# Scores of three row blocks in one TensorE visit, and values in one tile of 576 columns

## The chip, the cores and the metric

The kernel runs on one core of a Trainium2 chip. The metric is the device time of one execution in microseconds, as the median of several runs. Each core has a matrix engine (TensorE, PE), three engines for elementwise work (VectorE or DVE, ScalarE or ACT, GpSimd or POOL) and a queue engine (SyncE, SP) that only issues DMAs here. Each engine takes its instructions in the order in which they are laid out and waits at semaphores for the others. TensorE writes to PSUM alone, eight banks of 512 fp32 columns over 128 partitions.

## The reference

Forgetting attention (causal softmax attention with a decay of the scores) is followed by a bilinear feed-forward network (FFN):

```python
B, H, S, D = 8, 8, 576, 64
scores = (q @ k.T) / 8 + cum[:, :, :, None] - cum[:, :, None, :]   # cum = cumsum(log(clip(f)))
scores = where(causal, -1e9, scores)                                # above the diagonal
attn = exp(scores - max); attn /= sum(attn)
x = (attn @ v) put as (B * S, H * D)                                # 4608 tokens of 512
out = ((x @ w_a) * (x @ w_b)) @ w_out                               # d_ff = 1536
```

## The kernel before

**Work.** All of it is on one core, in fp16 with fp32 sums. Attention goes by pairs of heads: pair t covers batch t // 4 and heads t % 4 and t % 4 + 4, so there are 32 pairs. A pair's 576 query rows are four blocks of 128 (0 to 3) and a last one of 64 (block 4, both heads in one tile). Block i needs 128 (i + 1) columns of keys a head.

**Stages of a pair.** TensorE computes scores (`qk_group`). For blocks 0 to 3 it uses 64-row matmuls, the two heads in the two halves of the array (64\*128 in the profile); for block 4 of later pairs it uses queries laid out over 128 rows (64 columns wide, 128\*64). VectorE adds the decay and takes the row minimum of the negated sum in one custom operation (`do_decay`, L580) from PSUM into a buffer S. ScalarE takes the exponential with its row sum (`do_exp`, L611 and L607). VectorE takes reciprocals, GpSimd normalizes (`do_norm`, L629). SyncE's queue issues DMA transposes of the weights: PA (blocks 0 to 2) into PTA and PB (blocks 3 and 4) into PTB (`do_tr`, L643). TensorE multiplies them with the values (`do_pv` for blocks 0 to 3, L671, `do_pv4` for the last 64 rows, L687), and VectorE evicts the result into xT (L267 and L698). Batch 0 and, in part, batch 1 (pairs 0 to 7) go by other paths: their decay is added by TensorE or in other layouts, and transposes go through TensorE (`psP`).

**FFN.** Tokens go in groups of 256, 256, 256, 384, six of 512, and 384. Each of the twelve 128-column blocks of d_ff takes eight matmuls for `psa` and eight for `psb` (128\*64, two halves of the array); ScalarE copies `psa`, VectorE multiplies `psb` with it into `ht`. Then `pso` sums twelve blocks per 128 tokens; it is copied and stored. A group can start when the values of its batches stand in xT.

**PSUM before.** `sc` has two tiles of two banks, for scores, taken in turn. `pv` is one bank for values. `ff` is a ring of three banks for psa, psb, pso and the results of TensorE's transposes (psT for q and k, psP), in an order given by the table `FFBANK`. The last 64 value columns of pair t - 2 are written into spare columns of pair t's first score tile, so values of pair t - 2 stand behind pair t's first scores and are evicted in two parts (512 and 64 columns).

**Order.** All operations are objects with dependencies; `ORDER` lists them in one sequence written out by hand or by a planner, and each engine gets its share of it. `CHOICE` says, for operations that may run on one of several engines, which takes them. 24 operations `wake` (four matmuls each) on TensorE fill gaps at the start.

The lines in question before:

```python
c = ps.tile([128, 2, 512], FP32, tag="sc", bufs=2, name=f"sc{g}")           # L454, scores of one group
for gs in ([(0,), (1,), (2, 3)] if b in EARLY else [(0,), (1,), (2,), (3,)]):   # L757
pv = ... do_pv(old, (0, 1, 2, 3), {"A", "B"}), do_pv4(old, T.pop(("spare", t)))  # L790, old = t - 2
groups = [(1, 0), (2,), (3,), (4,)]                                         # L700
```

Of the kernel before, what the change touches and what calls it, by code (L numbers as in the profile page):

```python
# [25 lines left out]
def kernel(  # L26
# [76 lines left out]
    def paddings():  # L103
# [6 lines left out]
        for i in range(2):  # L110
# [13 lines left out]
            "sc": 2, "qd": 2, "pv": 1, "ff": 3}  # L124
# [54 lines left out]
    def f_tiles():  # L179
        x = [s_pool.tile([128, 1024], FP32, tag="S", name=n) for n in ("cum_f", "cum_l")]  # L180
        cw["f"], cw["l"] = (t[:, 0:S] for t in x)
        cw["1"] = x[0][:, S:].bitcast(FP16)[:, 0:S]
# [39 lines left out]
    for n in range(24):  # L222
        o = Op("PE", 0.427, lambda _: wake(2), [o_i], prio=-290, mode="full", name=f"wake{n}")
        o.prev = [last_wake] if n else []
        last_wake = o
        take(o, "pv")
# [42 lines left out]
    def load_v(b, sbs):  # L269
        x = T[("v32", b, sbs[0])] = n32_pool.tile([128, 2 * TG * 64], FP32, tag="n32", name="v32")  # L270
# [11 lines left out]
    def load_qk(b, which, half):  # L282
# [3 lines left out]
        if b in EARLY:  # L286
            if b == 0 and half:
                n = 2 * TG * 64
                x = wout16.rearrange("p n k -> p (n k)")[:, n * (which == "q"):n * (which == "q") + n]
                x = x.rearrange("p (j t d) -> p j t d", j=2, t=TG)  # L290
            else:
                x = n16_pool.tile([128, 2, TG, 64], FP16, tag="n16", name=f"{which}16")
# [3 lines left out]
        x = n32_pool.tile([128, 2 * TG * 64], FP32, tag="n32", name=f"{which}32")  # L296
# [4 lines left out]
    def cast_qk(e, b, which, half, lo, hi):  # L301
        key = ("n16", which, b, half)
        if key not in T:
            T[key] = n16_pool.tile([128, TG, 2, 64], FP16, tag="n16", name=f"{which}16")
# [145 lines left out]

    def qk_group(t, g):
        b, pr = divmod(t, NP)
        qT, kT = T[("T", "q", b)], T[("T", "k", b)]
        c = ps.tile([128, 2, 512], FP32, tag="sc", bufs=2, name=f"sc{g}")  # L454
# [28 lines left out]
        if g == 0:  # L483
            T[("spare", t)] = c[:, 0, 448:512]
# [64 lines left out]
    def do_max(t, i):  # L549
        if ("st", t) not in T:  # L550
            T[("st", t)] = st_pool.tile([128, 32], FP32, tag="st", name="st")
# [4 lines left out]
    def do_decay(t, g, i, h):  # L556

        if ("st", t) not in T:
            T[("st", t)] = st_pool.tile([128, 32], FP32, tag="st", name="st")
        if ("S", t, g) not in T:  # L560
            T[("S", t, g)] = s_pool.tile([128, 1024], FP32, tag="S", name="S")
# [9 lines left out]
        else:  # L571
            n = 128 * (i + 1)
            o, x, y = T[("z", t, i)][:, h * n:h * n + n], T[("s", t, i)][:, h, :], c[:, h, SM:SM + n]
# [16 lines left out]
    def p_blocks(t, i):  # L590
# [3 lines left out]
        else:  # L594
            if ("P", "A", t) not in T:
                T[("P", "A", t)] = p_pool.tile([128, 12, 128], FP16, tag="PA", bufs=RING["PA"], name="PA")
# [61 lines left out]
    def do_pv(t, rows, parts):  # L658
# [3 lines left out]
        o = ps.tile([128, 512], FP32, tag="pv", bufs=1, name="pv")  # L662
# [13 lines left out]
    def do_pv4(t, o=None):  # L676
# [4 lines left out]
        own = o is None  # L681
        if own:
            o = ps.tile([128, 512], FP32, tag="pv", bufs=1, name="pv4")[:, 0:64]
        T[("pv4", t)] = o
        for j in range(NSB):
            for h in range(2):
                nc.tensor.matmul(out=o[HP[h], :], lhsT=vt[:, j, pr + NP * h, :],  # L687
                                 rhs=pb[:, 8 + j, 64 * h:64 * h + 64], start=own and (j == 0),
                                 stop=(j == NSB - 1), skip_group_check=True)

# [24 lines left out]

    LAG = 2

    def attention(t, base):
# [36 lines left out]
        qk_of, sc_of, spare_pv = {}, {}, []  # L755
        qk_prev = None
        for gs in ([(0,), (1,), (2, 3)] if b in EARLY else [(0,), (1,), (2,), (3,)]):  # L757
# [5 lines left out]
            def stage(_, gs=gs):  # L763
                for g in gs:
# [11 lines left out]
            elif qk_prev:  # L776
                qk.deps.append(qk_prev)
            elif b not in EARLY and (t - 1, 3) in qk_ops:
                qk.prev.extend([qk_ops[(t - 1, 2)], qk_ops[(t - 1, 3)]])
            qk_prev = qk  # L780
            for g in gs:
                qk_of[g], sc_of[g] = qk, take(qk, "sc")
# [4 lines left out]
            old = t - LAG  # L787
            if gs == (0,) and b not in EARLY and old // NP not in EARLY:
                pv = Op("PE", 10 * 128 * COLS * 1.05 + 0.15,
                        lambda _, old=old: (do_pv(old, (0, 1, 2, 3), {"A", "B"}), do_pv4(old, T.pop(("spare", t)))),  # L790
                        [qk, *late[old][0]], prio=prio(0), mode="col", name=f"pv{old}")
                sc_of[0].append(pv)
                spare_pv.append(pv)
                late[old][1](pv, sc_of[0])
        direct_ex = {}
        for g, gi in [(g, groups[g]) for g in ((0, 1, 3, 2) if t in MASKP else (0, 1, 2, 3))]:
            qk, sc, su = qk_of[g], sc_of[g], None
            for i in gi:
                part = part_of(t, i)
                mxs = []  # L800
                for h in range(1 if direct else 2):
# [6 lines left out]
                    if g == 0 and spare_pv:  # L808
                        spare_pv[0].deps.append(mx)
# [15 lines left out]
                    sc.append(mx)  # L825
# [89 lines left out]
        def pv_late(pv, sc0):  # L915
            pvu = take(pv, "pv")
            p = pv.prio - 1
            ev = Op("DVE", 0.69, lambda e: do_ev(e, t, (0, 1, 2, 3)), [pv], prio=p, name=f"ev{t}")
            pvu.append(ev)
            ev4 = Op("DVE", 0.22, lambda _: do_ev4(t), [pv], prio=p)  # L920
            sc0.append(ev4)
# [3 lines left out]
            for i in range(NSB):  # L925
                ev_ops[(t, i)] = ev4 if i == 4 else ev

        if b not in EARLY and t + LAG < NP * B:
            late[t] = [o for x in sorted(trs) for o in trs[x]] + v_ops[b], pv_late
            return  # L930
        for rows in ([(0, 1), (2, 3)] if b in EARLY else [(0, 1, 2, 3)]):
# [6 lines left out]
            pvu = take(pv, "pv")  # L938
# [9 lines left out]
        pvu4 = take(pv4, "pv")  # L948
        ev4 = Op("DVE", 0.22, lambda _: do_ev4(t), [pv4], prio=p - 1)
# [15 lines left out]
    def ff_copy(e, t0, n, fb):  # L965
        a16 = a16_pool.tile([128, 512], FP16, tag="a16", name="a16")
# [3 lines left out]
    def ff_mul(t0, n, fb):  # L970
        ht = ht_pool.tile([128, 512], FP16, tag="ht", name="ht")
# [12 lines left out]
    def ff_ocopy(e, t0, tb):  # L984
        osb = osb_pool.tile([128, 512], FP32, tag="osb", name="osb")
# [3 lines left out]
    def last_copy(e, t0, tb, part):  # L989
        x = T[("half", part)] = s_pool.tile([128, 1024], FP32, tag="S", name="half")  # L990
# [86 lines left out]
    for n in cuts:  # L1077
# [3 lines left out]
        0 1 45 2 49 28 29 4-8 46 9 10 30-33 36 37 47 48 50 51 35 38 34 39 11 53 57 3 78 61 65 63 42 54  # L1081
# [6 lines left out]
        104 272 233 72 142 103 386 1750-1752 145 1753 201 202 150 1754-1757 108 25 146 151 1758 387 1760  # L1088
# [9 lines left out]
        339 438 368 361 362 494-496 314 315 320 505 488 500 1803 1804 373 1805 506 360 489 497 363 364  # L1098
# [156 lines left out]
```

## Time and profile before

| | us |
|---|---|
| median of 3 runs | 405.65 |
| lowest and highest | 405.36, 406.97 |
| profiled execution, its own time | 406.14 |
| its span, first to last instruction | 404.4 |
| TensorE busy | 389.1 (96%) |
| VectorE busy | 298.2 (74%) |
| ScalarE busy | 283.6 (70%) |
| GpSimd busy | 262.3 (65%) |

The profile names groups by line, engine, operation, and output and input tiles: `sc<-kT,qT` are scores, `psT` transposes of q and k, `pv<-PTA,nv` and `pv<-PTB,nv` values, `sc<-PTB,nv` the last 64 value columns in the spare part of a score tile, `psa`, `psb` and `pso` the FFN. A timeline line gives the start, the length, the engine, the line, the operation, the shape (for TensorE rows\*columns of the weights, then the moving operand) and the count; in square brackets stand idle time before it and what ended it. Matmuls are pipelined, so that lengths overlap and starts are the better measure. A line of waits gives microseconds in total, times, and the longest.

### The profile page before, as it was taken

Reading aid. Unit: us, or ns where it says so; the run is one execution under the profiler, and the core shown is the slowest. Engines: PE = TensorE matmul, PEld = TensorE weight load, DVE = VectorE, ACT = ScalarE, POOL = GpSimd, SP = SyncE. Lnnn points to the kernel's source line nnn. Section 1 sums busy time; section 2 is a strip of 40 time slices with the busy share of each in tenths; the row PEclk is TensorE's granted clock in tenths of the full one; section 3 lists DMA queues with packets and bytes.
Section 4 is the critical chain, followed back from the end, with each engine's and each line's share of the span. In section 5 each row is a group of like instructions: output and inputs, shape, how many; then the busy total and the mean of one; then the engine's idle time right before and its main releaser. Section 6 shows DMA issues by size and latency. Waiting matters only on the chain.

```text
span 404.4 us, 14858 instructions
## 1 busy us (share of the span) xinstructions
PE 389.1 (96%) x5792; PEld 240.6 (60%) x5792; DVE 298.2 (74%) x1003; ACT 283.6 (70%) x801; POOL 262.3 (65%) x489
## 2 busy tenths in 40 slices
PE   6899799999999999999999997999999999999995
PEld 2457586877956656555555554555555555555663
DVE  3777888999888888876897786788979882541331
ACT  2998889989988778887786867587788762231330
POOL 8897579968789687967698756875786573000000
PEclk9999999999999999999999999999999999999999
DMA  8999968999999999999999999999996496101102
GB/s 141 218 176 178 192 144 178 218 261 278 285 208 216 302 229 231 282 237 228 243 252 275 227 182 296 186 247 229 225 226 140 85 191 141 67 2 53 54 2 78
DMA packets 147190, 76.88 MB, mean 190 GB/s; under 512 B 124336, under 2 KB 129200, under 8 KB 147120
## 3 DMA queue, kind: packets, MB, share of 16 engines
q1 hardware_dynamic: 141040, 68.73, 76.9%
q0 software_dynamic: 5936, 7.08, 10.7%
q8 instruction: 45, 0.74, 0.8%
q14 instruction: 25, 0.20, 0.2%
q10 hardware_dynamic: 144, 0.13, 0.1%
HBM read 52.05 MB, written 9.58 MB: 152 GB/s over the span
## 4 chain that ended last, share of the span: by engine, by line
PE 65%; DMA 3%; DVE 2%; ACT 0%; issue 0%; ACTq 0%; DVEq 0%
PE pso L74 19%; PE psa L74 18%; PE psb L74 18%; PE sc L457 4%; PE pv L671 3%; DMA PTB<-PB 2%; PE sc L74 1%; PE psT L315 1%; DMA out_dram<-osb 1%; DVE S L580 1%; PE sc L687 1%; DVE osb L267 0%; DVE ht L972 0%; ACT osb L263 0%; DVE half L267 0%
## 5 line engine op out<-in xcount | busy, mean ns | idle before, releaser
L580 DVE CUSTOM_DVE_ANT_0 S<-sc,spread 64x576 f32<-64x576 f32 (+4 forms) x232 | 125.4, 562 | 14.0 <-PE sc L457 4.0
L74 PE MATMUL psa<-xT,wa 128*64 128x512 f16 (+2 forms) x1056 | 116.6, 342 | 1.8 <-DVE qT L265 1.3
L74 PE MATMUL psb<-xT,wb 128*64 128x512 f16 (+2 forms) x1056 | 116.3, 341 | 0.0
L263 ACT CAST a<-psa 128x512 f16<-128x512 f32 (+2 forms) x132 | 66.6, 504 | 59.2 <-PE psa L74 49.4
L629 POOL TENSOR_SCALAR PA<-PA,st 128x128 f16<-128x128 f16 (+2 forms) x192 | 89.8, 478 | 24.8 <-DVE st L621 16.0
L972 DVE TENSOR_TENSOR ht<-psb,a 128x512 f16<-128x512 f32 (+2 forms) x132 | 77.2, 589 | 33.5 <-PE psb L74 28.7
L74 PE MATMUL pso<-wout,ht 128*64 128x512 f16 x864 | 100.8, 380 | 0.0
L611 ACT ACTIVATE PA<-S,st 128x256 f16<-128x256 f32 (+2 forms) x168 | 84.4, 504 | 6.4 <-DVE st L580 6.0
L629 POOL TENSOR_SCALAR PB<-PB,st 128x512 f16<-128x512 f16 (+1 forms) x96 | 67.5, 710 | 21.6 <-DVE st L619 9.5
L74 PEld LDWEIGHTS <-wa 128*64 128x64 f16 x1056 | 58.3, 110 | 35.6 <-issue 4.5
L74 PEld LDWEIGHTS <-wb 128*64 128x64 f16 x1056 | 58.0, 110 | 31.6 <-issue 1.9
L74 PEld LDWEIGHTS <-ht 128*64 128x64 f16 x864 | 47.0, 110 | 37.5 <-issue 1.0
L611 ACT ACTIVATE PB<-S,st 128x512 f16<-128x512 f32 x56 | 40.1, 718 | 2.7 <-DVE st L580 2.4
L457 PE MATMUL sc<-kT,qT 64*128 64x128 f16 (+4 forms) x384 | 33.8, 266 | 1.5 <-ACT qT L261 1.1
L611 ACT ACTIVATION_READ_ACCUMULATOR PA<-S,st 128x1 f32 x168 | 32.0, 190 | 0.0
L267 DVE CAST xT<-pv 128x512 f16<-128x512 f32 (+1 forms) x40 | 23.0, 575 | 10.2 <-PE pv L671 10.1
L607 ACT ACTIVATE PB<-S,st 128x576 f16<-128x576 f32 x28 | 21.6, 772 | 9.5 <-POOL PA L629 5.7
L671 PEld LDWEIGHTS <-nv 128*64 128x64 f16 x640 | 21.9, 110 | 8.8 <-issue 4.4
L457 PEld LDWEIGHTS <-qT 64*128 64x128 f16 (+1 forms) x384 | 13.1, 95 | 19.8 <-issue 12.0
L580 DVE CUSTOM_DVE_ANT_1 S<-sc,spread 128x256 f32<-128x256 f32 x48 | 19.7, 419 | 5.3 <-PE sc L457 2.2
L263 ACT COPY osb<-pso 128x512 f32<-128x512 f32 x18 | 10.3, 575 | 18.2 <-PE pso L74 18.2
L580 DVE DVE_READ_ACCUMULATOR2_ANT st<- 128x1 f32 (+1 forms) x280 | 22.9, 82 | 0.0
(100 smaller groups left out, 465.1 us busy)
## 6 DMA issues: line engine op xcount, KB each, us to landing
spread<-cum_d SPq DMA_DIRECT2D x24, 576.0 KB, 6.3
out_dram<-osb SPq DMA_DIRECT2D x35, 256.0 KB, 3.4
v<-in_v_dram SPq DMA_DIRECT2D x32, 256.0 KB, 5.0
q<-in_q_dram SPq DMA_DIRECT2D x12, 576.0 KB, 5.4
k<-in_k_dram SPq DMA_DIRECT2D x12, 576.0 KB, 5.9
wout<-in_moe_w_out_dram POOLq DMA_DIRECT2D x3, 512.0 KB, 7.2
v<-in_v_dram SPq DMA_DIRECT2D x8, 128.0 KB, 7.5
wa<-in_moe_w_a_dram POOLq DMA_DIRECT2D x2, 512.0 KB, 8.7
```

The costliest lines, as they stand in the source:

```text
L74: nc.tensor.matmul(out=out[r], lhsT=lhsT[:, r], rhs=rhs, **kw)
L263: nc.scalar.copy(out=out_, in_=in_)
L267: VEC[e].tensor_copy(out=out_, in_=in_)
L315: nc.tensor.matmul(out=p[m][HP[j] if b in EARLY else slice(0, 128), 64 * t:64 * t + 64], lhsT=x[r, j, t, :] if b in EARLY else x[r, t, :], ...
L457: nc.tensor.matmul(out=dst, lhsT=lhsT, rhs=rhs, start=start, stop=stop, skip_group_check=True)
L580: nc.vector.tensor_tensor_reduce(out=o, in0=x, in1=y, scale=-1.0, scalar=3e38, op0=ADD, op1=MIN, accum_out=m)
L607: nc.scalar.activation(out=p_blocks(t, 4), in_=T[("s" if direct else "z", t, 4)], func=EXP, bias=st[:, 8:9], scale=sign, accum_out=st[:, 1 ...
L611: nc.scalar.activation(out=p_blocks(t, i)[:, :, h, :], in_=(T[("s", t, i)][:, h, :] if direct else T[("z", t, i)][:, h * n:h * n + n]).rea ...
L629: VEC[e].tensor_scalar(out=p, in0=p, scalar1=st[:, c:c + 1], scalar2=1.0, op0=MUL, op1=MUL)
L671: nc.tensor.matmul(out=o[HP[h], 128 * i:128 * i + 128], lhsT=vt[:, j, pr + NP * h, :], rhs=pt[:, base_blk[i] + 2 * block_at(t, i, j) + h, ...
L687: nc.tensor.matmul(out=o[HP[h], :], lhsT=vt[:, j, pr + NP * h, :], rhs=pb[:, 8 + j, 64 * h:64 * h + 64], start=own and (j == 0), stop=(j = ...
L972: nc.vector.tensor_tensor(out=ht[:, 0:n], in0=T.pop(("psb", t0, fb))[:, 0:n], in1=T.pop(("a16", t0, fb))[:, 0:n], op=MUL)
```

## The change

From batch 2 on (pairs 8 to 31):

- `qk_first` computes the scores of blocks 0, 1 and 2 in one visit of ten matmuls. Blocks 0 and 2 stand in a two-bank `sc` tile, one bank a head, and block 1 in two `ff` ring banks, one a head. Block 3 and block 4 keep a tile and a visit each.
- Values of all 576 columns go into one two-bank `sc` tile (`do_pv_all`), are no longer tied to the first scores two pairs on, and are evicted by one operation (`do_ev_all`), on VectorE or ScalarE as `CHOICE` says: 9 on VectorE, 15 on ScalarE.
- The separate `pv` bank goes; the `ff` ring has four banks, which `wake` and the values of pairs 0 to 7 use too.
- Which buffer a tile takes is read from tables (`SLOTS`) for PSUM and for S, PA, n32, n16, st, a16, ht and osb, instead of turn about. The counts of these buffers stay.
- `ORDER` and `CHOICE` are new throughout. Among GpSimd's instructions the first two loads of w_b stand ahead of the k and q loads of batch 1.

```diff
     def wake(n):
-        x = ps.tile([128, 512], FP32, tag="pv", bufs=1, name="wake")
+        x = ff_tile([128, 512], FP32, "wake")
...
-            "sc": 2, "qd": 2, "pv": 1, "ff": 3}
+            "sc": 2, "qd": 2, "ff": 4}
...
-    ff_bank = []
+    SLOTS = """
+        PA:03210231023102310231023102310231;S:010101011010101001010101010101010100101110000100101010111101011100
...
+    """
+    slot_of = {x.split(":")[0]: list(x.split(":")[1]) for x in "".join(SLOTS.split()).split(";") if x}
+
+    def slot(p, shape, dtype, tag, name):
+        return p.tile(shape, dtype, tag=tag + slot_of[tag].pop(0), bufs=1, name=name)
 
     def ff_tile(shape, dtype, name):
-        return ps.tile(shape, dtype, tag=f"ff{ff_bank.pop(0)}", bufs=1, name=name)
+        return slot(ps, shape, dtype, "ff", name)
...
+    def qk_first(t):
+        b, pr = divmod(t, NP)
+        qT, kT = T[("T", "q", b)], T[("T", "k", b)]
+        c = slot(ps, [128, 2, 512], FP32, "sc", "sc0")
+        c1 = [ff_tile([128, 512], FP32, f"sc1{h}")[:, 0:256] for h in range(2)]
+        out_of = {0: [c[:, h, 0:128] for h in range(2)], 1: c1, 2: [c[:, h, 128:512] for h in range(2)]}
+        for i in (1, 0, 2):
+            for x, (j0, j1) in enumerate(key_runs(t, i)):
+                for h, r in enumerate(HP):
+                    w, col = 128 * (j1 - j0), 128 * x
+                    nc.tensor.matmul(out=out_of[i][h][:, col:col + w], lhsT=qT[r, pr, 128 * i:128 * i + 128],
+                                     rhs=kT[r, pr, 128 * j0:128 * j1], start=i < 2 and x == 0 , stop=True,
+                                     skip_group_check=True)
+        for i in range(3):
+            T[("s", t, i)] = out_of[i]
...
-        if g == 0:
-            T[("spare", t)] = c[:, 0, 448:512]
...
+    def do_pv_all(t):
+        o = T[("pvx", t)] = slot(ps, [128, 2, 512], FP32, "sc", "pvx").rearrange("p a k -> p (a k)")
+        do_pv(t, (0, 1, 2, 3), {"A", "B"}, o)
+        do_pv4(t, o[:, SF:S])
+
+    def do_ev_all(e, t):
+        b, pr = divmod(t, NP)
+        cast(e, xT[pr][:, b, :], T.pop(("pvx", t))[:, 0:S], False)
...
-    LAG = 2
...
-        for gs in ([(0,), (1,), (2, 3)] if b in EARLY else [(0,), (1,), (2,), (3,)]):
+        for gs in ([(0,), (1,), (2, 3)] if b in EARLY else [(0, 1), (2,), (3,)]):
...
+            if gs == (0, 1):
+                u = take(qk, "sc")
+                users_of.update({0: u, 2: u, 1: (take(qk, "ff"), take(qk, "ff"))})
...
-            old = t - LAG
-            if gs == (0,) and b not in EARLY and old // NP not in EARLY:
-                pv = Op("PE", 10 * 128 * COLS * 1.05 + 0.15,
-                        lambda _, old=old: (do_pv(old, (0, 1, 2, 3), {"A", "B"}), do_pv4(old, T.pop(("spare", t)))),
-                        [qk, *late[old][0]], prio=prio(0), mode="col", name=f"pv{old}")
...
+        if b not in EARLY:
+            p = prio(0) - 1
+            pv = Op("PE", 0.7, lambda _: do_pv_all(t), [o for x in sorted(trs) for o in trs[x]] + v_ops[b], prio=p, mode="col", name=f"pv{t}")
+            pvu = take(pv, "sc")
+            ev = Op(None, {"DVE": 0.75, "ACT": 0.78}, lambda e: do_ev_all(e, t), [pv], prio=p, name=f"ev{t}")
...
-            pvu = take(pv, "pv")
+            pvu = take(pv, "ff")
...
     ORDER = """
...
     CHOICE = """
...
-    FFBANK = """
...
```

More of the change, by code (lines that the diff above doesn't have):

```diff
@@ L179, in f_tiles @@
     def f_tiles():
-        x = [s_pool.tile([128, 1024], FP32, tag="S", name=n) for n in ("cum_f", "cum_l")]
+        x = [slot(s_pool, [128, 1024], FP32, "S", n) for n in ("cum_f", "cum_l")]
         cw["f"], cw["l"] = (t[:, 0:S] for t in x)
@@ L291, in load_qk @@
             else:
-                x = n16_pool.tile([128, 2, TG, 64], FP16, tag="n16", name=f"{which}16")
+                x = slot(n16_pool, [128, 2 * TG * 64], FP16, "n16", f"{which}16").rearrange("p (j t d) -> p j t d", j=2, t=TG)
             T[("n16", which, b, half)] = x
@@ L295, in load_qk @@
             return
-        x = n32_pool.tile([128, 2 * TG * 64], FP32, tag="n32", name=f"{which}32")
+        x = slot(n32_pool, [128, 2 * TG * 64], FP32, "n32", f"{which}32")
         x = x.rearrange("p (j t d) -> p j t d", j=2, t=TG)
@@ L303, in cast_qk @@
         if key not in T:
-            T[key] = n16_pool.tile([128, TG, 2, 64], FP16, tag="n16", name=f"{which}16")
+            x = slot(n16_pool, [128, 2 * TG * 64], FP16, "n16", f"{which}16")
+            T[key] = x.rearrange("p (t h d) -> p t h d", t=TG, h=2)
         cast(e, T[key][:, lo:hi].rearrange("p t h d -> p h t d"), T[("n32", which, b, half)][:, :, lo:hi, :], which == "q")
@@ L680, in do_pv4 @@
         vt = nv[b % 2]
-        own = o is None
-        if own:
-            o = ps.tile([128, 512], FP32, tag="pv", bufs=1, name="pv4")[:, 0:64]
+        if o is None:
+            o = ff_tile([128, 512], FP32, "pv4")[:, 0:64]
         T[("pv4", t)] = o
@@ L775, in attention @@
                 qk.deps.append(cp)
-            elif qk_prev:
+            elif b in EARLY and qk_prev:
                 qk.deps.append(qk_prev)
-            elif b not in EARLY and (t - 1, 3) in qk_ops:
-                qk.prev.extend([qk_ops[(t - 1, 2)], qk_ops[(t - 1, 3)]])
             qk_prev = qk
+            if gs == (0, 1):
+                u = take(qk, "sc")
+                users_of.update({0: u, 2: u, 1: (take(qk, "ff"), take(qk, "ff"))})
             for g in gs:
-                qk_of[g], sc_of[g] = qk, take(qk, "sc")
+                qk_of[g] = qk
+                if gs != (0, 1):
+                    u = take(qk, "sc")
+                    users_of.update({i: u for i in groups[g]})
                 qk_ops[(t, g)] = qk
@@ L925, in pv_late @@
             for i in range(NSB):
-                ev_ops[(t, i)] = ev4 if i == 4 else ev
-        if b not in EARLY and t + LAG < NP * B:
-            late[t] = [o for x in sorted(trs) for o in trs[x]] + v_ops[b], pv_late
+                ev_ops[(t, i)] = ev
             return
-        for rows in ([(0, 1), (2, 3)] if b in EARLY else [(0, 1, 2, 3)]):
+        for rows in [(0, 1), (2, 3)]:
             parts = {part_of(t, i) for i in rows}
@@ L989, in last_copy @@
     def last_copy(e, t0, tb, part):
-        x = T[("half", part)] = s_pool.tile([128, 1024], FP32, tag="S", name="half")
+        x = T[("half", part)] = slot(s_pool, [128, 1024], FP32, "S", "half")
         cast(e, x[:, 0:256], T[("pso", t0, tb)][:, 256 * part:256 * part + 256], False)
```

127 lines of the change are left out of this document (67 added, 60 removed), and 178 rows, old and new, of the table ORDER.

## The prediction

> **What bounds the kernel now.** I read the page first, then the busy times by stretch, TensorE's waits, its timeline, and the chain that ended last.
>
> ```profile
> span 404.4 us, 14858 instructions
> PE 389.1 (96%) x5792; PEld 240.6 (60%) x5792; DVE 298.2 (74%) x1003; ACT 283.6 (70%) x801; POOL 262.3 (65%) x489
> PEclk9999999999999999999999999999999999999999
> PE 65%; DMA 3%; DVE 2%; ACT 0%; issue 0%; ACTq 0%; DVEq 0%
> ```
>
> TensorE (PE) is busy 96% of the span, always at full clock, and is nearly all of the chain that ended last. Where it is not busy, the stretches show:
>
> ```profile
> core 0: us, PE busy (x) PEld busy (x) DVE busy (x) ACT busy (x) POOL busy (x), PEclk, DMA share, GB/s
> 0.00:20.00 20.00, 14.84 (x278) 7.32 (x278) 11.71 (x27) 12.49 (x35) 17.32 (x51) 1.00 1.02 179
> 20.00:50.00 30.00, 26.97 (x592) 18.87 (x586) 24.60 (x62) 25.97 (x77) 23.38 (x41) 1.00 1.04 179
> 120.00:160.00 40.00, 40.00 (x598) 25.06 (x594) 33.30 (x122) 32.35 (x93) 31.32 (x57) 1.00 1.11 248
> 240.00:280.00 40.00, 37.84 (x516) 21.47 (x514) 31.44 (x115) 29.36 (x85) 28.24 (x51) 1.00 1.04 236
> 360.00:380.00 20.00, 20.00 (x198) 11.47 (x196) 5.44 (x9) 4.47 (x8) 0.00 (x0) 1.00 0.14 53
> ```
>
> Of the 15.3 us idle, 8.2 lie in the first 50 us and about 4 behind the last matmul; in the long middle TensorE stands still once, at 240 to 280. VectorE (DVE), the busiest of the others, has 33.3 of 40 us there. So TensorE's order sets the pace, and an edit is worth what it takes from TensorE's own time, plus the waits that it opens or closes:
>
> ```profile
> PE wake L74 <- POOL ident masks.py:199: 2.9, 1, 2.9
> PE pv L671 <- DMA PTB<-PB: 2.1, 1, 2.1
> PE psa L74 <- DVE qT L265: 1.3, 1, 1.3
> PE pv L671 <- issue: 1.2, 1, 1.2
> PE sc L457 <- ACT qT L261: 1.1, 2, 0.9
> ```
>
> **Part 1: the visits.** "Busy" hides a loss, and the timeline shows it by its start times (the durations overlap):
>
> ```profile
> 195.59 1.06 PE L74 MATMUL psa<-xT,wa 128*64 128x512 f16 x8
> 196.58 0.51 PE L457 MATMUL sc<-kT,qT 64*128 64x128 f16 x10
> 197.01 1.05 PE L74 MATMUL psb<-xT,wb 128*64 128x512 f16 x8
> 197.90 1.03 PE L74 MATMUL psa<-xT,wa 128*64 128x512 f16 x8
> 198.76 1.03 PE L74 MATMUL psb<-xT,wb 128*64 128x512 f16 x8
> ...
> 104.35 0.34 PE L457 MATMUL sc<-kT,qT 64*128 64x128 f16 x4
> 104.52 0.43 PE L315 MATMUL psT<-ident,q 64*128 64x64 f16 x18
> ...
> 112.56 0.34 PE L457 MATMUL sc<-kT,qT 64*128 64x128 f16 x6
> 112.74 0.43 PE L315 MATMUL psT<-ident,k 64*128 64x64 f16 x18
> ```
>
> An FFN product of eight matmuls takes 0.86 us when its own kind follows (197.90 to 198.76). Four score matmuls take 0.17 us (104.35 to 104.52) and six 0.18, where other 64-row work follows. From 195.59 to 197.90 lie two products (1.73) and ten score matmuls (0.35), that is 2.08 us of work in 2.31: going over to the 64-row shape and back costs 0.23 us a visit.
>
> In TensorE's order of instructions I counted how often 64-row work (scores of blocks 0 to 3, transposes of q and k) begins behind 128-row work: 82 times before and 68 after, of which 55 and 44 from pair 8's first scores on. Blocks 0, 1 and 2 now come as one visit of ten matmuls where they were often two (six and four). The number of matmuls is the same in both, 5,792, so nothing else of TensorE's work changes. Eleven visits in the paced stretch give 11 x 0.23 = 2.5 us. The other three lie where TensorE also waits for others; they are worth 0 to 0.7, and I take 0.4, since the stretch from 20 to 50 us is already 90% busy. Sum: -2.9 us, with ends at -2.5 and -3.2. [...]
>
> Values and the last rows' scores cost no such switch:
>
> ```profile
> 190.07 1.03 PE L74 MATMUL psb<-xT,wb 128*64 128x512 f16 x8
> 190.94 0.33 PE L671 MATMUL pv<-PTA,nv 128*64 128x128 f16 x6
> ...
> 191.65 1.03 PE L74 MATMUL psa<-xT,wa 128*64 128x512 f16 x8
> ```
>
> The product before them lasts 0.87, and all thirty value matmuls take 0.71 us. One 576-column tile holds the same thirty: 0 on TensorE.
>
> **Part 2: where values stand, and the one long wait.**
>
> ```profile
> 244.03 0.36 PE L671 MATMUL pv<-PTA,nv 128*64 128x128 f16 x6
> 246.45 0.25 PE L671 MATMUL pv<-PTB,nv 128*64 128x128 f16 x2 [2.06 <-DMA PTB<-PB]
> ...
> 237.43 8.97 DMA PTB<-PB
> ```
>
> Pair 21's values start at 244.03, and their transposed second half lands only at 246.4: the 2.1 us above. Before, values of a pair had to follow the first scores two pairs on, because their last 64 columns lay in those scores' tile. The change drops that tie. Counting FFN groups of eight matmuls between a pair's last scores and its values, the order has 19.5 on average (18 for pair 21, least 12) before, and 25.0 (25 for pair 21, least 16) after. Seven more groups at 0.86 are 6 us of cover for a wait of 2.1, so I take the wait as gone: -2.1, with ends 0 (the softmax of the pair slips as far) and -2.1. Pair 31, with 12 groups, had no such wait, so 16 to 35 should do. What is late next, where values come later, is the FFN that needs them: in the counted order the last values of a batch stand between one and four product groups ahead of the first FFN product on that batch's rows, before between one and eight. One group, 0.86, just covers an eviction of 0.64 to 0.75 (below), so I put no price on it beyond the new waits of part 3.
>
> **Part 3: banks and evictions.** The separate value bank becomes a fourth ring bank, but each pair now takes two ring banks for block 1, and values take a two-bank score tile.
>
> ```profile
> L580 DVE CUSTOM_DVE_ANT_1 S<-sc,spread 128x256 f32<-128x256 f32 x48 | 19.7, 419 | 5.3 <-PE sc L457 2.2 <-issue 1.5 <-ACT PB L611 1.0
> L267 DVE CAST xT<-pv 128x512 f16<-128x512 f32 x24 | 16.3, 681 | 7.8 <-PE pv L671 7.8
> L698 DVE CAST xT<-sc 128x64 f16<-128x64 f32 x22 | 4.9, 222 | 6.7 <-PE sc L687 6.4
> L263 ACT COPY kT<-psT 128x576 f16<-128x576 f16 x26 | 15.8, 641 | 3.7 <-PE psT L315 3.5
> L267 DVE COPY kT<-psT 128x576 f16<-128x576 f16 x6 | 4.5, 750 | 0.3 <-PE psT L315 0.3
> ```
>
> VectorE loses two evictions a pair (0.681 and 0.222) and gets 9 of the 24 new ones, at about 0.75 by the nearest row of 576 columns; ScalarE gets 15 at about 0.64. That is 24 x 0.90 - 9 x 0.75 = 15 us less on VectorE and 15 x 0.64 = 10 more on ScalarE. Both lie beside TensorE's work: 0 on the path, and if that cover were gone, 0.64 to 0.75 a pair. A block-1 bank is free after its 419 ns pass. What is queued behind the wait for it is the FFN product, transposes or scores that take that bank next, and everything after them on TensorE. In the order, the tightest block-1 tile has 0.7 us of TensorE work before its bank is wanted again, counted by the durations of what stands between; but FFN tiles already lived with 0.77 before. I expect some short new waits, and bound them by 0 and by the one long wait of the old order, 2.1; I take the middle, +1.0. The scratch and output buffers (S, PA, n16, ht and so on) keep their count and go by a table instead of turn about: 0, since no engine instruction comes with it, and the waits that it could shift are in the same +1.0.
>
> **Part 4: the start.** GpSimd now issues two wb loads (256 and 512 KB) ahead of the first k and q of batch 1:
>
> ```profile
> k<-in_k_dram POOLq DMA_DIRECT2D x3, 288.0 KB, 5.3
> wb<-in_moe_w_b_dram POOLq DMA_DIRECT2D x2, 512.0 KB, 7.1
> ```
>
> Both k and q are transposed just before pair 0's blocks 3 and 4, some 10 us after their issue, against 5.3 us to land, or up to 12.4 if they queue wholly behind wb. The transposes keep TensorE in order, so a late q holds those scores. On the other side, the q transposes of batch 1's second half are now followed by transposes that do not take their bank, where the old order had 1.3 us of FFN waiting for the qT eviction. I take 0, between -2.5 (the waits of 1.3 and 1.2 both go) and +2 (the late load).
>
> **The sum.** -2.9 - 2.1 + 1.0 + 0 = -4.0 us against the profiled execution: span 404.4, its own time 406.14, hence 402.1. The median of the runs shown, 405.65, is 0.5 below that execution, so I forecast 401.6 us.
>
> **The rivals.**
>
> - *The gain is hidden.* TensorE leaves its visits sooner, but the softmax of the next pair arrives as before, so the time shows up as waits on transposes. For it: the wait at 244 shows that the pair's pipeline can be the later one. Against it: VectorE at 33.3 of 40 has room. Then only the three visits ahead of pair 8 are won, 3 x 0.23 = 0.7 us: 404.9.
> - *The bound moves to the block-1 banks (slower).* Scores of block 1 come in a ring bank, and each of the 24 visits then holds TensorE for a decay pass, 0.42 us, since VectorE takes its work in order and may be at another operation of 0.7. For it: 0.7 us of cover at the tightest place. Against it: VectorE gets 15 us lighter. Price 24 x 0.42 = 10.1, less the 5.0 gained: +5.1, so 410.7. It decides from 5.0 / 24 = 0.21 us a visit upward. [...] The trace of before does not bear that out (33.3 of 40 on VectorE), hence a chance below one in five.
> - *More goes than I count.* The early waits of 1.3 and 1.2 vanish too, and no new ones come: -2.9 - 2.1 - 2.5 = -7.5, so 398.1. For it: the q transposes are no longer followed by a product that takes their bank. Against it: the first 50 us also wait for the softmax of batch 0, which has the same instructions in both.
>
> **How the numbers follow.** Likeliest case 0.50, hidden 0.18, slower rival 0.18, larger gain 0.14. A measurement of this kernel tells about 0.5% (2 us) from no change. Faster than 403.6: 0.50 + 0.14 plus a little of the hidden case, 0.66. Within 403.6 to 407.7: 0.16. Slower: 0.18. The range for 8 in 10 takes in the larger gain and the hidden case and stops below the slower one: 398.0 to 406.5.
>
> **What would show it.** Visits: right if, in the timeline of after, ten scores of blocks 0 to 2 stand together and products on either side keep 0.99 and 0.89 from start to start; wrong if a product behind them starts over 0.3 us late with a decay pass as its releaser. Values: right if no row of TensorE's waits names a PTA or PTB transfer. Banks: right if waits on VectorE and ScalarE past 50 us sum to about 1 us. Start: right if the first FFN product starts within 1.5 us of before. The prediction is wrong if the softmax pipeline, which I did not time pair by pair, runs later in the new order than the cover that I counted.

## The result, and the profile after

| | before | after |
|---|---|---|
| median of 20 executions, us | 405.89 | 408.47 |
| lowest and highest, us | 404.35, 407.8 | 406.18, 410.6 |
| profiled execution, its own time | 406.14 | 408.91 |
| its span | 404.4 | 407.2 |
| first FFN product starts | 33.75 | 40.73 |
| last matmul ends | 400.34 | 403.45 |

The changed kernel takes 1.0061 times as long (95% interval 1.0041 to 1.0081): slower by 0.6%, where 401.6 us was forecast. The page of the profile after, in the lines that answer to those shown of before (span; busy time of each engine; TensorE's clock in 40 slices; the chain that ended last):

```profile
span 407.2 us, 14765 instructions
PE 388.6 (95%) x5792; PEld 249.4 (61%) x5792; DVE 288.0 (71%) x969; ACT 288.1 (71%) x812; POOL 260.4 (64%) x488
PEclk9996999999999999999999999999999999999999
PE 80%; issue 5%; POOL 4%; DMA 4%; ACT 3%; DVE 3%; SPq 0%; POOLq 0%; DVEq 0%; ACTq 0%
```

TensorE has the same 5,792 matmuls in nearly the same busy time (389.1 before). New is one slice with the clock at six tenths, near the start. Busy time by stretch (PE, PEld, DVE, ACT, POOL, then TensorE's clock, DMA share, GB/s):

```profile
0.00:20.00 20.00, 15.46 (x280) 8.16 (x282) 13.49 (x29) 13.42 (x39) 16.58 (x50) 1.00 1.02 178
20.00:50.00 30.00, 21.89 (x470) 15.31 (x468) 17.83 (x42) 18.94 (x56) 18.54 (x36) 0.89 0.99 172
240.00:280.00 40.00, 39.12 (x528) 23.37 (x526) 30.89 (x113) 31.49 (x92) 32.28 (x59) 1.00 1.02 218
```

From 20 to 50 us TensorE is busy 21.89 us at a clock of 0.89, where it had 26.97 at 1.00. TensorE's waits name the place, and its timeline the sequence (start, length, what, and in brackets the idle time ahead and what ended it). First the waits of after, then GpSimd's and TensorE's timeline of after, then GpSimd's first cast of values and the first FFN products of before:

```profile
PE psP L74 <- POOL PA L663: 7.5, 1, 7.5
PE pvx L706 <- DMA PTB<-PB: 0.8, 1, 0.8
PE pvx L706 <- DVE st L614: 0.6, 1, 0.6
```

```profile
33.87 1.04 POOL L284 CAST nv<-v 128x1024 f16<-128x1024 f32 x1 [7.99 <-DMA v<-in_v_dram]
35.30 0.75 PE L74 MATMUL psP<-ident,PA 128*64 128x128 f16 x10 [7.45 <-POOL PA L663]
40.73 0.60 PE L74 MATMUL psa<-xT,wa 128*64 128x256 f16 x8
```

```profile
20.35 1.05 POOL L267 CAST nv<-v 128x1024 f16<-128x1024 f32 x1
33.75 0.60 PE L74 MATMUL psa<-xT,wa 128*64 128x256 f16 x8
34.19 0.60 PE L74 MATMUL psb<-xT,wb 128*64 128x256 f16 x8
```

GpSimd stands at a cast of values for 7.99 us until a load lands, where the same cast ran at 20.35 us without a wait before; the norms of PA are queued behind that cast; TensorE's transposes of PA wait 7.45 us for the norms. The first FFN product comes 7.0 us later. SyncE's queue shows why the load is late. First before, then after:

```profile
2.49 8.98 SPq L274 DMA_DIRECT2D v<-in_v_dram  x5
11.59 3.43 SPq L213 DMA_DIRECT2D cum_d<-cum_f  x2
```

```profile
2.49 3.60 SPq L291 DMA_DIRECT2D v<-in_v_dram  x3
10.48 0.82 SPq L230 DMA_DIRECT2D cum_d<-cum_f  x2
11.34 33.05 SPq L291 DMA_DIRECT2D v<-in_v_dram  x7
```

Before, all five loads of batch 0's values go out from 2.49 us. In the new order only three do; the two halves of blocks 0 and 1, which the cast needs, stand behind the store of `cum_d`, which goes out at 10.48 us. They go out from 11.34 us, among the weight loads of GpSimd's queue, and the first of them (256 KB) takes 12.8 us to land. From 20 to 26 us of after the two queues look like this (packets, MB, share of 16 engines; q0 is GpSimd's queue, q1 SyncE's):

```profile
q0 software_dynamic: 968, 0.96, 94.8%
q1 hardware_dynamic: 809, 0.20, 25.7%
```

In these 6 us the two queues moved about as many packets (968 and 809), but a packet of the queue with the values held 0.25 KB and one of GpSimd's queue 1 KB, so the queue with the values moved 0.20 MB beside 0.96. From 12 to 20 us of the same execution the counts were 918 and 1,620 (1.19 and 0.53 MB), so that equal counts are no rule here; what decides between the queues was not shown.

The rest of the kernel did get shorter. I laid the bare duration of each kind of TensorE work (start to start among neighbours that don't wait) against its start times, from the first FFN product to the last matmul, in the two profiles and in a second one of each kernel (last two experiments):

| us | before | before, second | after | after, second |
|---|---|---|---|---|
| bare work | 346.3 | 346.3 | 346.1 | 346.1 |
| single losses over 0.16 us, up to 85 us | 3.8 | 4.5 | 0.7 | 0.7 |
| the same, past 85 us | 3.3 | 2.3 | 3.8 | 3.1 |
| small losses (shape changes and the like) | 13.2 | 13.1 | 12.1 | 12.4 |
| sum | 366.6 | 366.1 | 362.7 | 362.4 |
| first FFN product | 33.8 | 33.6 | 40.7 | 40.3 |

The sums and the starts are read off the traces; how a sum divides into rows depends on which durations are called bare. With other bare durations (for each kind, half the median time from a matmul to the next but one) the early losses are 4.1 and 4.6 against 1.2 and 1.2, but those past 85 us are 3.3 and 1.8 in both kernels: the early gain is clear, the growth past 85 us is not.

So, as means of the two pairs, the new order wins 3.8 us behind the start and loses 6.8 at the start. The gain does not come from the late start: in experiment 1, where the first product is on time, the same stretch takes 363.2 us.

### The profile page after: what moved, and what is told of

It is laid out like the page before. It is cut to its first block, busy times and chain, and to the rows that moved or that the text cites. A ratio compares the mean times of both kernels' runs of the same rounds, so it can differ in the third digit from the quotient of the medians.

```text
span 407.2 us, 14765 instructions
## 1 busy us (share of the span) xinstructions
PE 388.6 (95%) x5792; PEld 249.4 (61%) x5792; DVE 288.0 (71%) x969; ACT 288.1 (71%) x812; POOL 260.4 (64%) x488
## 4 chain that ended last, share of the span: by engine, by line
PE 80%; issue 5%; POOL 4%; DMA 4%; ACT 3%; DVE 3%; SPq 0%; POOLq 0%; DVEq 0%; ACTq 0%
PE psa L74 22%; PE psb L74 22%; PE pso L74 18%; PE sc L491 4%; PE pvx L706 3%; POOL PA L663 2%; PE psP L74 2%; PE psT L333 2%; PE sc L479 2%; DMA v<-in_v_dram 1%; PE sc L74 1%; DMA out_dram<-osb 1%; DMA cum_f<-in_f_dram 1%; PE pv L706 1%; DVE S L614 1%
## 5 line engine op out<-in xcount | busy, mean ns | idle before, releaser
L74 PE MATMUL pso<-wout,ht 128*64 128x512 f16 x864 | 102.3, 380 | 0.0
L1007 DVE TENSOR_TENSOR ht<-psb,a 128x512 f16<-128x512 f32 (+2 forms) x132 | 75.9, 589 | 37.2 <-PE psb L74 31.6
L663 POOL TENSOR_SCALAR PA<-PA,st 128x256 f16<-128x256 f16 (+2 forms) x192 | 89.4, 476 | 15.1 <-DVE st L655 13.2
L74 PEld LDWEIGHTS <-wb 128*64 128x64 f16 x1056 | 62.8, 110 | 29.8 <-issue 1.3
L74 PEld LDWEIGHTS <-wa 128*64 128x64 f16 x1056 | 61.5, 110 | 29.2 <-issue 3.2
L74 PEld LDWEIGHTS <-ht 128*64 128x64 f16 x864 | 48.8, 110 | 34.2 <-issue 2.1
L645 ACT ACTIVATE PB<-S,st 128x512 f16<-128x512 f32 x56 | 40.3, 721 | 6.8 <-DVE st L614 6.0
L571 POOL TENSOR_SCALAR_AFFINE_SELECT spread<-spread 128x768 f32<-128x768 f32 x24 | 20.8, 865 | 13.6 <-DMA spread<-cum_d 12.2
L284 POOL CAST nv<-v 128x1024 f16<-128x1024 f32 (+1 forms) x23 | 20.4, 887 | 11.1 <-DMA v<-in_v_dram 11.0
L284 DVE COPY osb<-pso 128x512 f32<-128x512 f32 x17 | 11.7, 688 | 18.4 <-PE pso L74 18.4
L655 DVE RECIPROCAL st<-st 128x2 f32<-128x2 f32 x128 | 18.8, 156 | 6.9 <-ACT PB L645 4.3
```

Source lines behind the costliest of these rows:

```text
L74: nc.tensor.matmul(out=out[r], lhsT=lhsT[:, r], rhs=rhs, **kw)
L284: VEC[e].tensor_copy(out=out_, in_=in_)
L571: nc.gpsimd.affine_select(out=c[:, :, 0:SM].rearrange("p h (j k) -> p h j k", k=128), in_=c[:, :, SM:2 * SM].rearrange("p h (j k) -> p h j ...
L645: nc.scalar.activation(out=p_blocks(t, i)[:, :, h, :], in_=(T[("s", t, i)][:, h, :] if direct else T[("z", t, i)][:, h * n:h * n + n]).rea ...
L655: nc.vector.reciprocal(out=st[:, 20 + 2 * i:22 + 2 * i], in_=st[:, 10 + 2 * i:12 + 2 * i])
L663: VEC[e].tensor_scalar(out=p, in0=p, scalar1=st[:, c:c + 1], scalar2=1.0, op0=MUL, op1=MUL)
```

## The experiments

Each expectation stood before the run. "Product" is the start of the first FFN product. All but the last two were timed in rounds beside the kernel before, at 406.1 us for the first four and 405.71 for the next four.

**1. The load ahead of the store.**

```diff
-        44 78 258 262 280 63 65 42 61 54 123 12 13 55 ...
+        44 78 258 262 280 63 65 61 42 54 123 12 13 55 ...
```

> One load moves on SyncE's queue of the changed kernel: the values of batch 0, blocks 0 and 1, are issued ahead of the store of cum_d instead of behind it; nothing else changes on any engine. Theory A (the start lost 7.0 us because this load came late): its first half lands by 16 us and its second by 20 us instead of 24 and 34, GpSimd's cast no longer waits 8.0 us, the first FFN product starts at 33.5 to 35 us instead of 40.7, the clock in 20 to 50 us is 1.00 instead of 0.89, and the time is 400.5 to 402.5 us, that is 6 to 8 below the changed kernel and 1.0% below the kernel before. Rival B (the weight loads on the other queue hold the values wherever they stand on this one): the second half still lands after 28 us, and the time is 404.5 to 407 us. Rival C (the start does not matter, since the later work waits for something else): the first product starts early and the time stays within 1 us of 408.5.

402.59 us (401.26 to 408.48 over 12 executions), ratio to before 0.992 (0.989 to 0.995). The timeline of GpSimd and TensorE, then the stretch from 20 to 50 us:

```profile
27.87 1.04 POOL L284 CAST nv<-v 128x1024 f16<-128x1024 f32 x1 [0.35 <-DMA v<-in_v_dram]
33.94 0.60 PE L74 MATMUL psa<-xT,wa 128*64 128x256 f16 x8
```

```profile
20.00:50.00 30.00, 28.54 (x659) 20.88 (x654) 25.64 (x67) 26.80 (x80) 23.45 (x45) 1.00 1.14 195
```

Theory A by product, clock and (within 0.1) time: one place in one queue takes back 5.9 us, and the changed kernel is then faster than the one before. But the values, issued at 6.1 and 7.4 us, still land at 21.2 and 27.7 us, not by 16 and 20, and the cast still waits 0.35 us. That part is close to rival B's, and five of the twelve executions took 404.7 us or more, two of them 408.3 and 408.5, as long as the changed kernel. By the landing times the early weight loads alone still hold the values; the five long executions themselves were not profiled.

**2. The cast behind the norms.** The load stays late; GpSimd's cast (operation 62) moves behind five norms.

```diff
-        ... 265 333 334 62 137 221 220 227 226 100 23 154 155 105
+        ... 265 333 334 137 221 220 227 226 62 100 23 154 155 105
```

> The changed kernel with the late load left as it is; GpSimd's cast of those values (the one that waited 8.0 us) stands behind the five norms that it stood ahead of. Theory A1 (the load is late, but it holds TensorE only through GpSimd's queue, in which the norms stand behind the cast): TensorE's wait of 7.5 us for the norms goes, the first FFN product starts at 34 to 36 us, and the time is 401 to 404 us. Rival A2 (the values themselves are wanted then, so that the wait only moves from the norms to the first values): the first product starts early, a wait of 3 us or more appears ahead of pair 0's to 2's values, and the time is 405 to 408.5 us.

407.28 us, ratio 1.0017 (0.9991 to 1.0042). TensorE's waits, then its timeline:

```profile
PE pv L706 <- POOL nv L284: 3.9, 1, 3.9
```

```profile
37.49 0.60 PE L74 MATMUL psa<-xT,wa 128*64 128x256 f16 x8
```

Rival A2: the wait for the norms is gone and a wait of 3.9 us for the values themselves has taken its place. GpSimd's queue passed the lateness on early; it did not make it. The median fell by 1.2 us; the profiled execution (404.45 us) was the fastest of ten.

**3. The weight loads later.** The load stays behind the store; operations 70 and 74 (wb) go behind the two wa loads 68 and 69.

```diff
-        ... 34 41 57 3 70 74
-        44 78 258 262 280 63 65 42 61 54 123 ...
+        ... 34 41 57 3 44 78 258 262 280 63 65 42 61 54 123 ...
-        127 133 ... 283 19 68 69 96 129 ...
+        127 133 ... 283 19 68 69 70 74 96 129 ...
```

> The changed kernel with the late load left behind the store of cum_d, but the two weight loads (wb, 256 and 512 KB) that GpSimd's queue has ahead of k and q of batch 1 stand behind the two wa loads. Theory A (the place on SyncE's queue alone makes the load late): the values still land at 30 to 34 us and the time stays within 1.5 us of 408.5. Rival B (the weight loads take the transfer engines from the values): the second half lands 3 us or more earlier, TensorE's wait of 7.5 us shrinks by as much, and the time is 402 to 405.5 us.

402.54 us, ratio 0.9911 (0.9876 to 0.9945). The cast no longer waits at all (timeline of this kernel), and the bytes of SyncE's queue from 12 to 20 us, of this kernel and then of after, show why:

```profile
25.74 1.03 POOL L284 CAST nv<-v 128x1024 f16<-128x1024 f32 x1
32.51 0.60 PE L74 MATMUL psa<-xT,wa 128*64 128x256 f16 x8
```

```profile
q1 hardware_dynamic: 2667, 0.79, 41.6%
```

```profile
q1 hardware_dynamic: 1620, 0.53, 34.0%
```

Rival B: with the load as late in its queue as in the changed kernel, 0.26 MB more of SyncE's data moves from 12 to 20 us, the first half of the values (issued at 11.34 us in both) lands in 4.3 us instead of 12.8, and nothing waits for them. So the place in SyncE's queue is not enough alone.

**4. The late load in the kernel before.**

```diff
-        ... 53 57 3 78 61 65 63 42 54
+        ... 53 57 3 78 65 63 42 61 54
```

> The kernel before, with this one step of the change put into it: the values of batch 0, blocks 0 and 1, are issued last of the three value loads and behind the store of cum_d. Theory A (this step alone makes the late start): the second half lands 10 us or more later than 13.3, the first FFN product starts 4 to 7 us later than 33.75, and the time is 409.5 to 412.5 us (405.9 + 4 to 7). Rival B (it is late only beside the weight loads that the change also moved forward on GpSimd's queue): the values land by 20 us, ahead of their cast, and the time stays within 1 us of 405.9.

406.26 us, ratio 1.0003 (0.9976 to 1.003). Rival B: no change. The first half of the values, issued at 11.15 us, lands at 15.7, and the cast runs at 20.1 us without a wait. The old order's first weight load goes out only at 13.74 us, after both halves and after k of batch 1.

**5. Both steps in the kernel before.** As in 4, with operations 70 and 74 moved up as well.

```diff
-        ... 53 57 3 78 61 65 63 42 54
+        ... 53 57 3 70 74 78 65 63 42 61 54
...
-        ... 96 129 97 70 62 130 ...
+        ... 96 129 97 62 130 ...
-        ... 143 73 268 74 384 64 ...
+        ... 143 73 268 384 64 ...
```

> The kernel before with both steps of the change's start: the values of blocks 0 and 1 issued behind the store of cum_d, and the two wb loads (256 and 512 KB) ahead of k and q of batch 1. Each theory says what the pair of them does where the first alone did nothing (406.3 beside 406.1). Theory A (the two together make the start late, whatever the rest of the order): the second half of the values lands after 25 us, GpSimd's cast waits 4 us or more for it, the first FFN product starts at 38 to 42 us, and the time is 409.5 to 413 us. Rival B (the late start belongs to the new order as a whole): the values land by 21 us and the time stays within 1.5 us of 406.

414.27 us, ratio 1.0203 (1.0164 to 1.0243): 8.6 us slower, 1.3 above the top of theory A's time. GpSimd's cast, TensorE's transposes of PA and product:

```profile
28.82 1.04 POOL L267 CAST nv<-v 128x1024 f16<-128x1024 f32 x1 [8.58 <-DMA v<-in_v_dram]
30.71 0.32 PE L74 MATMUL psP<-ident,PA 128*64 128x128 f16 x2 [7.54 <-POOL PA L629]
43.47 0.60 PE L74 MATMUL psa<-xT,wa 128*64 128x256 f16 x8
```

This is the chain of the changed kernel, made in the old order by these two steps and nothing else, so the rest of the new order isn't needed for the late start. The early wb loads alone were not tried in the old order; for the new order experiment 1 is that case.

**6. Both repairs in the changed kernel** (the edits of 1 and 3 together).

> Both repairs of the start together: the values of blocks 0 and 1 ahead of the store of cum_d, and the two wb loads behind the two wa loads. Theory A (the late start comes from the two together, so that either repair takes all of it): 401.5 to 403.5 us, the same as either alone within 1 us, first FFN product at 32 to 34.5 us. Rival B (each takes a part): 398 to 401 us, first product before 31.5 us. Rival C (weights that come later are then waited for): over 403.5 us with waits of 1 us or more on weights or scores between 30 and 50 us.

401.8 us (400.49 to 402.48), ratio 0.9893 (0.9858 to 0.9929); product at 32.75. Theory A: the same as either alone within 1 us. The values land at 16.0 and 16.7 us, 11 us sooner at the second half than in 1, which shows what the early wb loads did there. The product is 1.2 us earlier than in 1 and the profiled execution 1.0 us shorter (401.61 against 402.60). A new wait of 1.4 us stands at 43 us, for which the profile names no releaser; from the first product to the last matmul the kernel still needs only 363.4 us. What the pair of repairs adds is evenness: none of six executions over 402.5. This is the lowest median of the versions tried, 1.1% below the kernel before; beside experiments 1 and 3 the difference is within their intervals.

**7. Two visits in place of one.** On top of 1: from pair 8 on block 2's scores (four matmuls) come behind the next FFN product, in 22 of 24 pairs.

```diff
-        for i in (1, 0, 2):
+        for i in blocks:                    # (1, 0), and (2,) behind the next psa, psb or pso
```

> The kernel with the values issued ahead (402.6 us), but from pair 8 on block 2's scores are a visit of their own behind the next FFN product: 90 visits of 64-row work in place of 68, the same 5,792 matmuls. Theory A (a visit costs TensorE 0.21 us, so that the two visits which the change really saved are worth 0.4 us): 22 x 0.21 = 4.6 us more, 406.5 to 408, all of it in TensorE's start-to-start times around the new visits. Rival B (time saved at a visit comes back as a wait): within 1 us of 402.6. Rival C (the second visit also lets banks go earlier): 403.5 to 405.5, with fewer waits on VectorE and ScalarE.

412.66 us, ratio 1.0176 (1.0128 to 1.0223): no theory had its 10 us over experiment 1. TensorE's timeline at pair 20, of after and then of this kernel (the two 512-column score matmuls are pair 19's block 3):

```profile
204.58 1.03 PE L74 MATMUL psa<-xT,wa 128*64 128x512 f16 x8
205.54 0.51 PE L479 MATMUL sc<-kT,qT 64*128 64x128 f16 x10
205.89 0.38 PE L491 MATMUL sc<-kT,qT 64*128 64x512 f16 x2
206.20 1.05 PE L74 MATMUL psb<-xT,wb 128*64 128x512 f16 x8
207.08 1.03 PE L74 MATMUL psa<-xT,wa 128*64 128x512 f16 x8
```

```profile
208.24 1.03 PE L74 MATMUL psa<-xT,wa 128*64 128x512 f16 x8
209.20 0.34 PE L483 MATMUL sc<-kT,qT 64*128 64x128 f16 x6
209.38 0.38 PE L495 MATMUL sc<-kT,qT 64*128 64x512 f16 x2
209.69 1.05 PE L74 MATMUL psb<-xT,wb 128*64 128x512 f16 x8
210.68 0.34 PE L483 MATMUL sc<-kT,qT 64*128 64x128 f16 x4
210.94 1.05 PE L74 MATMUL psa<-xT,wa 128*64 128x512 f16 x8
211.83 1.03 PE L74 MATMUL psb<-xT,wb 128*64 128x512 f16 x8
PE sc L483 <- DVE st L618: 4.1, 3, 2.7
```

After: two products and one visit, 2.50 us. Here: three products and two visits of the same scores, 3.59 us. The third product is 0.86, which leaves 0.23 for the second visit. Over the whole stretch from the first product (here 37.55) to the last matmul this kernel needs 372.7 us against 363.2 of experiment 1. Of the 9.5, the small losses are 4.3 (22 x 0.195, near theory A's 0.21) and the longer waits 5.2, above all the new 4.1 us in which block 2's scores wait for a decay pass of VectorE. In the longest, 2.7 us, that is the pass over block 0 of the same pair, which stands in the same bank (it ends at 188.45, the scores start at 188.51). I had not thought of a split visit that waits in its second half. (In its profiled execution the values landed at 30.3 us and TensorE waited 3.6 us for norms of PA, with the same order at the start as in experiment 1: that start is a race.)

**8. Two value visits later.** On top of 1: pair 15's values behind two more FFN groups, pair 23's behind one.

```diff
-        1989 959 1994 1996 1997 890 2000 2001 891 ...
+        1989 959 1994 1996 1997 2000 2001 890 891 ...
-        ... 1251 1293 1294 2130 ... 1401 2138 1413 1397 1295 ...
+        ... 1251 1293 2130 ... 1401 2138 1294 1413 1397 1295 ...
```

> The kernel with the values issued ahead (402.6 us), with the value visits of pairs 15 and 23 moved behind later FFN groups, by two and by one. There TensorE waited 0.86 us for a score pass of VectorE that had the two-bank tile which the values now take, and 0.84 us for a PTB transfer. Theory A (the new waits are short and local: a group or two of cover closes them): both go, and the time is 400.7 to 401.9 us. Rival B (the FFN products that need these values then wait, since only one to four groups stand between): a wait of 0.5 us or more on an xT eviction appears behind each, and the time is 402.2 to 403.5 us.

403.29 us, ratio 0.9933 (0.9906 to 0.9959). Both waits on values are gone, and TensorE's timeline has instead:

```profile
183.86 0.40 PE L479 MATMUL sc<-kT,qT 64*128 64x128 f16 x6 [0.51 <-ACT xT L280]
266.96 0.49 PE L479 MATMUL sc<-kT,qT 64*128 64x128 f16 x9 [0.59 <-ACT osb L280]
```

Rival B in effect, though not as I put it: not the FFN waits, but the next scores, whose bank ScalarE has yet to empty. 1.7 us of waits went and no time was gained. At these two places, then, later values only move the wait to the next bank that isn't empty; the new waits are 1.1 us, and where the rest of the 1.7 went I did not separate.

**9 and 10. Both kernels unchanged, profiled again.**

> The kernel before, unchanged, profiled a second time. Theory A (the waits read in its profile belong to its order): TensorE waits again 1.5 to 2.5 us for a PTB transfer at pair 21's values (244 us), and about 3.8 us in all at 43 to 77 us. Rival B (single waits belong to the execution): the wait at 244 us is under 0.5 us, others stand elsewhere, and from the first FFN product to the last matmul the time is again 366 to 367.5 us.

> The changed kernel, unchanged, profiled a second time. Theory A (the late values belong to its order): GpSimd's cast waits 6 us or more for them, the first FFN product starts at 38.5 us or later, and the clock in 20 to 50 us is under 0.95. Rival B (the lateness was that one execution's): the first FFN product starts before 37 us. Either way the waits of 0.5 to 1 us for a decay pass near 185 us and for a PTB transfer near 270 us stand again if they belong to the order.

405.58 and 408.12 us, one execution each. The kernel before in the stretch that held the long wait; then two rows of the changed kernel's waits on TensorE:

```profile
240.00:280.00 40.00, 39.89 (x536) 22.66 (x534) 32.95 (x119) 30.63 (x89) 28.83 (x52) 1.00 1.00 242
```

```profile
PE psP L74 <- POOL PA L663: 6.7, 1, 6.7
PE pvx L706 <- DMA PTB<-PB: 0.4, 1, 0.4
```

For the kernel before, rival B: no wait at 244 us (39.89 of 40 busy, against 37.84), yet from first product to last matmul it needs 366.1 us instead of 366.6. The early losses stand again (4.5 us), as theory A had it. For the changed kernel, theory A: product at 40.26, clock 0.89. Of its later waits the one near 270 us came back at half its size; the one near 185 us did not, but a wait of 0.36 us for a decay pass stood at 146 us.

## Why the prediction was wrong, point by point

- **Part 4, the start, is the step that failed.** It was priced 0, with ends -2.5 and +2; it measured +7.0 (+6.6 in the second pair of profiles). I weighed the two wb loads against k and q on the same queue, where the traces show no harm worth naming (waits on q of 0.7 us). The harm came through another queue. The load of blocks 0 and 1 had been moved behind the store of `cum_d` on SyncE's queue, and neither the list of the change nor the prediction mentions that move. With both steps the load is late (experiment 5). The place behind the store costs nothing alone, in the new order (3) or the old (4). The early wb loads alone do hold the values: in the new order the second half lands at 27.7 us (1) and 30.3 (7) against 16.7 with both repairs (6), and five of the twelve executions of 1 were 2.6 us or more above the median of the other seven. None of those five was profiled; the 3.6 us wait of 7, which has the same start, is the likeliest cause. The bound of +2 was taken from k and q and did not cover the values.
- **Part 1, the visits: the price was right, the count wrong.** A visit costs 0.195 to 0.23 us (experiment 7), as forecast. But "82 times before" should have been 70: in 12 places I took the last 64 value columns for scores, since they are written into a score tile. The second profile of before shows such a place, where the first ten matmuls have the shape of the FFN:

```profile
246.24 0.35 PE L687 MATMUL sc<-PTB,nv 128*64 128x64 f16 x10
246.52 0.34 PE L457 MATMUL sc<-kT,qT 64*128 64x128 f16 x4
```

  With 70 against 68 the term is 2 x 0.2 = -0.4, not -2.9, and from pair 8's first scores on, where eleven visits were to be saved, it is 43 before and 44 after. Visits that begin with scores did fall, from 58 to 43, but the transposes of q and k now begin 25 visits where they began 12. All small losses together fell by 0.7 to 1.1; what makes up the rest of that I did not separate.
- **Part 2, the long wait: gone as forecast, but it was no term of the sum.** The 2.1 us belonged to one execution. The kernel before runs as long without it. And by the sign that the prediction set (no wait on a PTA or PTB transfer) the cover is not enough: 0.8 and 0.4 us on PTB remain.
- **Part 3, the banks: +1.0 was of the right kind.** In the profiles of after the waits on VectorE and ScalarE past 50 us sum to 1.2 and 1.3, as the prediction's sign asked. Losses past 85 us went from 3.3 and 2.3 to 3.8 and 3.1 by the table above, so that parts 2 and 3 together, forecast at -1.1, came to +0.5 and +0.8; by the other count they came to nothing. The values' new two-bank tile does wait for decay passes, as the rival on banks had it, but by tenths of a microsecond and not at every pair.
- **The early waits, the end -2.5 of part 4,** did go: 3.8 and 4.5 us up to 85 us became 0.7. The gain is not in every run: in experiments 3, 6 and 8, whose first product is earlier still, a wait of 1.2 to 1.7 us stands at 43 us. That the q transposes no longer have a product behind them that takes their bank is my reason for the gain, and was not tried by itself.
- **The sum behind the start** was forecast at -4.0 and measured -3.9 and -3.8. That is no success of its terms: one real gain that I had put down as an end stands in for two that weren't there. The rivals were about these terms as well; none of them dealt with a late load at the start.

## What to carry to other kernels

When an order is rewritten, list for each queue which loads have moved past which, and for each moved load its first user and what is queued behind that user: here 256 KB of values, in packets of 0.25 KB, took 12.8 us to land with the two wb loads early on the other queue, against 4.3 with them later (experiment 3). Before a wait from one profile is entered as a gain, look for it in a second profile of the same kernel. And count shape changes by the shape in the rows, not by the name of the tile that is written.

## What the runs showed of the hardware that I had not expected

- From 20 to 26 us of after, GpSimd's queue and SyncE's moved 968 and 809 packets, but 0.96 and 0.20 MB; from 12 to 20 us they moved 918 and 1,620 packets, 1.19 and 0.53 MB.
- The late load alone cost the old order nothing (ratio 1.0003), and with the early wb loads 8.6 us; in the new order the removal of either step gave back about 6 us in the median (402.59 and 402.54 against 408.47), though with the early wb loads left in, five of twelve executions stayed at 404.7 or more.
- TensorE's clock fell during the long wait of after: 7.45 us idle up to 35.30 us, with the clock at 0.97 from 28 to 32 us, 0.50 from 32 to 38, 0.85 from 38 to 40 and 1.00 from 40 on (0.89 over 20 to 50). Experiment 4 has no such wait, the longest there is 1.6 us, and its clock fell too, to 0.94 over 20 to 50 us, and the first FFN product took its eight matmuls at half speed, in 0.86 us instead of 0.44 (33.75 to 34.19 of before). What sets off such a fall was not shown. Experiment 4's stretch, then its timeline:

```profile
20.00:50.00 30.00, 27.89 (x554) 19.49 (x557) 22.65 (x58) 24.23 (x72) 22.74 (x41) 0.94 1.06 176
```

```profile
32.87 0.35 PE L315 MATMUL psT<-ident,q 64*64 64x64 f16 x21 [1.62 <-issue]
35.31 1.07 PE L74 MATMUL psa<-xT,wa 128*64 128x256 f16 x8
36.17 1.07 PE L74 MATMUL psb<-xT,wb 128*64 128x256 f16 x8
```
